# Two reorderings in a fused linear-attention and cosine-gated MLP kernel: an O unit for an F part behind Y of pair 3, and k conversion and T of pair 10 some steps later

## Chip, cores, metric

One core of a Trainium2 chip. The metric is the device time of one launch in microseconds (us), lower is better. All profiles are of that one core.

## The reference, cut to what matters

```python
# q, k, v: (4, 8, 768, 64) fp32; w_in: (512, 2048); w_out: (2048, 512)
for t in range(S):                                   # per batch and head
    state = gamma * state + outer(k[t], v[t])
    y[t] = scale * q[t] @ state
x = y.transpose(0, 2, 1, 3).reshape(3072, 512)
h = x @ w_in
out = (h * cos(h)) @ w_out
```

The kernel does the recurrence in chunks of 128 steps. A *pair* is one chunk of two batches; there are 12, numbered from 0. Two pairs make a *group* of 512 tokens for the MLP. The names used below:

- **conv_k, conv_q, conv_v**: fp32 to bf16, q and v with the decay factors; k on ScalarE, q and v on GpSimd.
- **T**: transposes of q and k, from pair 3 on by DMA.
- **A**: scores of a pair, 16 matmuls into four PSUM banks; VectorE then masks them (`am`).
- **Y, S**: output of the recurrence from masks and state; ScalarE copies it to `xt`. S is the state update.
- **F**: `x @ w_in`, cosine on ScalarE (`cosb`), product on VectorE (`gt`). An F part is 8 matmuls of 128x256, half of what one pair needs for one r, a quarter of `w_in`'s columns; an F unit is 4 of 128x512. From group 2 on a group has 16 steps, each with one F unit.
- **O**: `gt @ w_out`, four units of 4 matmuls make one output tile.

## The kernel before: the parts concerned

```python
banks = Banks([... for i in range(7)], clk)          # seven PSUM banks, one more holds the state
cosb = [sb([128, 4 * C], BF16, f"cosb{i}") for i in range(3)]

def conv_k(p, on_act):
    for b in range(2):
        if on_act:
            nc.scalar.copy(out=qk[p % NB][:, b, 1], in_=kf[SLOT[p]][b])
    ...

def act(bank, out):
    cb = cosb[f_no[0] % 3]                           # cosine buffers in turn
    f_no[0] += 1
    nc.scalar.activation(out=cb, in_=bank, func=AF.Sin, bias=halfpi)
    ...
    nc.vector.tensor_tensor(out=out, in0=bank, in1=cb, op=ALU.mult)
    ...

    # group 1
    pair_f(2, 0)
    conv_k(4, True)
    pair_f(2, 1)
    conv_k(5, True)
    attend(3)                                        # A and masks of pair 3
    cq(4); stage_t_dma(4); cq(5); stage_t_dma(5); cv(4); cv(5)
    fetch_two(6)
    pair_f(2, 2)
    pair_f(2, 3, (0,))
    stage_y(3, nc.scalar.copy)
    pair_f(2, 3, (1,))
    pair_f(3, 0)
    ...
    o_units(1, 0, 2)
    conv_k(6, True)
    attend(4)
    ...
    k_at = {(2, 4): 8, (2, 7): 9, (3, 0): 10, (3, 12): 11}      # (group, step): pair
    t_at = {(2, 8): (8, 9), (3, 2): (10,), (3, 13): (11,)}
    a_at = {(2, 2): 6, (2, 10): 7, (3, 2): 8}

    for g in range(2, NG + 1):
        for s in range(16):
            ...
            if g < NG:
                unit_f(g, s)
            ...  # O unit of the group before, put-off masks
            if at in k_at:
                conv_k(k_at[at], True)
            if at in t_at:
                for p in t_at[at]:
                    cq(p)
                    stage_t_dma(p)
                for p in t_at[at]:
                    cv(p)
                if at == (2, 8):
                    fetch_two(10)                    # loads k, q of 10, k, q of 11, v of 10, 11
            ...
```

## Time and profile before

| | before |
|---|---|
| timed runs | 210.12 us median of 3 (209.74 to 210.32) |
| profiled run | 209.16 us, span 207.2 us |
| TensorE busy, granted clock | 96% of the span, 1.0 |
| ScalarE, VectorE, GpSimd busy | 55%, 54%, 44% |

The granted clock is the share of full TensorE clock that the chip's throttle let through. TensorE is the bound: an engine busy for 96% of the span leaves only its few gaps to win. The prediction below shows the two gaps that the change is aimed at. Part 4 of the page, the chain that ended last, gives shares of the span by engine:

```profile
PE 47%; DMA 10%; POOL 7%; issue 4%; SPq 1%; ACT 1%; DVE 1%; POOLq 0%; ACTq 0%
```

Followed back from the end, the chain is TensorE's for half of the span and then leaves it for loads and GpSimd: somewhere TensorE's end time was set by data coming in, not by its own work. In the timeline lines below, a bracket at the end gives how long the engine stood idle before the instruction, and what ended that.

### The profile page before, as it was taken

What the parts mean: (1) busy time and instruction counts of PE and PEld (TensorE: products, weight loads), DVE (VectorE), ACT (ScalarE), POOL (GpSimd) and SP (SyncE); (2) the same over time, 40 slices, a digit from 0 to 9 for tenths busy, and PEclk for the clock granted to TensorE, in tenths of its full rate; (3) what the DMA queues carried; (4) which work ended last, traced back from release to release, by engine and by line L of the source; (5) the groups of instructions that cost most, each with busy time, mean ns of one, the idle gap of its engine ahead of it and who ended that gap; (6) DMA issues with size and microseconds to landing.
All of it is one profiled execution on the core that took longest, in us unless ns stands there. A gap on an engine that the chain in (4) does not pass through costs nothing.

```text
span 207.2 us, 4072 instructions
## 1 busy us (share of the span) xinstructions
PE 198.4 (96%) x1608; PEld 112.7 (54%) x1630; DVE 112.5 (54%) x186; ACT 114.9 (55%) x193; POOL 92.1 (44%) x99
## 2 busy tenths in 40 slices
PE   7889999999999999999989999999999999999994
PEld 2457554558896555556444465544465444444453
DVE  4792883643967445869574467754458244444000
ACT  6777872259986536787363556453554653554120
POOL 8999238499998389979831630000000000000000
PEclk9999999999999999999999999999999999999999
DMA  6999999989999978999999905101101101110212
GB/s 163 349 237 204 216 252 288 317 186 301 292 158 289 321 106 156 307 295 191 265 365 348 197 3 152 52 3 51 51 0 55 51 0 54 51 51 2 101 51 101
DMA packets 33571, 34.34 MB, mean 166 GB/s; under 512 B 23376, under 2 KB 25680, under 8 KB 33552
## 3 DMA queue, kind: packets, MB, share of 16 engines
q0 software_dynamic: 7824, 22.29, 38.9%
q1 hardware_dynamic: 24544, 11.44, 25.3%
q10 hardware_dynamic: 1184, 0.36, 0.7%
q8 instruction: 12, 0.20, 0.4%
q14 instruction: 7, 0.06, 0.1%
HBM read 27.26 MB, written 6.29 MB: 162 GB/s over the span
## 4 chain that ended last, share of the span: by engine, by line
PE 47%; DMA 10%; POOL 7%; issue 4%; SPq 1%; ACT 1%; DVE 1%; POOLq 0%; ACTq 0%
PE bank L387 24%; PE bank L340 19%; DMA vf<-in_v_dram 4%; DMA qf<-in_q_dram 3%; DMA out_dram<-ob 3%; POOL vs L204 2%; PE bank L407 2%; POOL qk L197 2%; POOL kf L137 2%; POOL qf L137 1%; PE bank L281 1%; PE bank L286 1%; PE bank L259 1%; SPq L380 0%; PE st_ps L303 0%
## 5 line engine op out<-in xcount | busy, mean ns | idle before, releaser
L333 DVE TENSOR_TENSOR gt<-bank,cosb 128x512 bf16<-128x512 f32 x96 | 65.1, 689 | 62.9 <-ACT cosb L329 62.5
L329 ACT ACTIVATE cosb<-bank,halfpi 128x512 bf16<-128x512 f32 x96 | 65.0, 687 | 48.2 <-PE bank L340 42.0
L387 PE MATMUL bank<-w_out_sb,gt 128*128 128x512 bf16 x359 | 88.5, 379 | 0.7 <-issue 0.3
L340 PE MATMUL bank<-xt,w_in 128*128 128x512 bf16 x294 | 74.2, 380 | 1.5 <-DVE gt L333 0.8
L387 PEld LDWEIGHTS <-gt 128*128 128x128 bf16 x368 | 35.5, 98 | 41.2
L340 PEld LDWEIGHTS <-w_in 128*128 128x128 bf16 x304 | 33.8, 114 | 31.6 <-issue 0.8
L268 DVE TENSOR_TENSOR am<-bank,mask 128x512 bf16<-128x512 f32 x48 | 30.4, 682 | 4.4 <-PE bank L259 4.4
L204 POOL TENSOR_TENSOR vs<-vf,gk 128x512 bf16<-128x512 f32 x21 | 21.4, 1049 | 11.6 <-DMA vf<-in_v_dram 8.3
L197 POOL TENSOR_TENSOR qk<-qf,gq 128x512 bf16<-128x512 f32 x18 | 18.4, 1044 | 9.6 <-DMA out_dram<-ob 4.4
L394 ACT COPY ob<-bank 128x512 f32<-128x512 f32 x23 | 13.4, 587 | 16.5 <-PE bank L387 16.3
L210 ACT CAST qk<-kf 128x512 bf16<-128x512 f32 x24 | 13.9, 617 | 12.2 <-DMA kf<-in_k_dram 9.7
L290 ACT CAST xt<-bank 128x512 bf16<-128x512 f32 x24 | 13.0, 589 | 7.1 <-PE bank L286 7.1
L351 PE MATMUL bank<-xt,w_in 128*128 128x256 bf16 x128 | 14.6, 273 | 0.0
L351 PEld LDWEIGHTS <-w_in 128*128 128x128 bf16 x128 | 13.8, 113 | 0.4
L286 PE MATMUL bank<-am,vs 128*64 128x128 bf16 x192 | 11.7, 220 | 0.4 <-DVE am L268 0.4
L281 PEld LDWEIGHTS <-stb 128*64 128x64 bf16 x160 | 8.7, 109 | 4.7 <-issue 4.3
L281 PE MATMUL bank<-qkt,stb 128*64 128x128 bf16 x160 | 10.7, 222 | 0.3 <-DVE am L268 0.3
L137 POOL DMA_DIRECT2D kf<-in_k_dram x9 | 10.6, 1174 | 0.0
L286 PEld LDWEIGHTS <-vs 128*64 128x64 bf16 x192 | 10.0, 110 | 0.5 <-issue 0.4
L315 DVE CAST stb<-st_ps 64x512 bf16<-64x512 f32 x12 | 8.2, 685 | 2.7 <-PE st_ps L303 2.6
L137 POOL DMA_DIRECT2D qf<-in_q_dram x8 | 9.2, 1154 | 0.0
L137 POOL DMA_DIRECT2D vf<-in_v_dram x8 | 9.2, 1152 | 0.0
(48 smaller groups left out, 98.6 us busy)
## 6 DMA issues: line engine op xcount, KB each, us to landing
out_dram<-ob SPq DMA_DIRECT2D x23, 256.0 KB, 2.6
kf<-in_k_dram POOLq DMA_DIRECT2D x9, 512.0 KB, 6.7
qf<-in_q_dram POOLq DMA_DIRECT2D x8, 512.0 KB, 7.1
vf<-in_v_dram POOLq DMA_DIRECT2D x8, 512.0 KB, 8.3
vf<-in_v_dram POOLq DMA_DIRECT2D x8, 256.0 KB, 5.6
w_out_sb<-in_moe_w_out_dram POOLq DMA_DIRECT2D x4, 512.0 KB, 12.2
qf<-in_q_dram POOLq DMA_DIRECT2D x6, 256.0 KB, 7.2
w_in<-in_moe_w_in_dram POOLq DMA_DIRECT2D x3, 512.0 KB, 8.2
```

Of the source, the lines that this page charges most:

```text
L137: nc.gpsimd.dma_start(out=both[n][SLOT[p]].rearrange("p b h d -> p (b h) d"), in_=SRC[n][1][2 * bp : 2 * bp + 2, :, ds(c * C, C)].rearrang ...
L197: eng.tensor_tensor(out=qk[p % NB][:, b, 0], in0=qf[SLOT[p]][b], in1=bc(gq, p % NC), op=ALU.mult)
L204: eng.tensor_tensor(out=vs[p % NB][:, b], in0=vf[SLOT[p]][b], in1=bc(gk, p % NC), op=ALU.mult)
L210: nc.scalar.copy(out=qk[p % NB][:, b, 1], in_=kf[SLOT[p]][b])
L268: nc.vector.tensor_tensor(out=am[p % 2][b][j], in0=ap[j], in1=mask.unsqueeze(1).to_broadcast([128, HP, 128]), op=ALU.mult)
L281: nc.tensor.matmul(yp[ts(j, 64), a, :], lhsT=stb[p % 2][:, b, a, ts(j, 64)], rhs=qt(n, b, a), start=True, stop=False, skip_group_check=True)
L286: nc.tensor.matmul(yp[ts(j, 64), a, :], lhsT=vs[n][:, b, 2 * a + j, :], rhs=am[p % 2][b][j][:, a, :], start=(c == 0), stop=True, skip_grou ...
L329: nc.scalar.activation(out=cb, in_=bank, func=AF.Sin, bias=halfpi)
L333: nc.vector.tensor_tensor(out=out, in0=bank, in1=cb, op=ALU.mult)
L340: nc.tensor.matmul(bank, lhsT=w_in_t(i, f), rhs=xt[g % 2][:, i, :], start=(i == 0), stop=(i == KIN - 1))
L351: nc.tensor.matmul(bank[:, ts(e, 256)], lhsT=w_in_t(i, f + e), rhs=xt[g % 2][:, i, ts(hf, 256)], start=(i == 0 and e == 0), stop=(i == KIN ...
L387: nc.tensor.matmul(bank, lhsT=gt[g % 2][:, f, ts(j, 128)], rhs=w_out_sb[:, f, :], start=(f == 0), stop=(f == KOUT - 1))
```

## The change

The intent: Y of pair 3 should not wait for its masks, and ScalarE should not stand in front of a k that has not landed while finished F units wait behind it.

```diff
     pair_f(2, 2)
-    pair_f(2, 3, (0,))
+    pair_f(2, 3)
     stage_y(3, nc.scalar.copy)
-    pair_f(2, 3, (1,))
+    unit_o(1, 0, 0)
     pair_f(3, 0)
@@
-    o_units(1, 0, 2)
+    o_units(1, 1, 2)
@@
-    k_at = {(2, 4): 8, (2, 7): 9, (3, 0): 10, (3, 12): 11}
-    t_at = {(2, 8): (8, 9), (3, 2): (10,), (3, 13): (11,)}
+    k_at = {(2, 4): 8, (2, 7): 9, (3, 5): 10, (3, 12): 11}
+    t_at = {(2, 8): (8, 9), (3, 6): (10,), (3, 13): (11,)}
```

The first two hunks are *part 1*, the last is *part 2*. Part 2 moves the conversion five steps later and T four.

## The prediction

> **What bounds the kernel now.** I read the page first, then who waited for whom on TensorE, then the timelines of TensorE, ScalarE and VectorE around the two edited places, the chain that ended last, and the landing times of single loads.
>
> ```profile
> PE 198.4 (96%) x1608; PEld 112.7 (54%) x1630; DVE 112.5 (54%) x186; ACT 114.9 (55%) x193; POOL 92.1 (44%) x99
> PEclk9999999999999999999999999999999999999999
> ```
>
> TensorE is busy 96% of a 207.2 us span at full clock; no other engine passes 55%. So the edit can only pay by removing time in which TensorE stands still. Its waits are few:
>
> ```profile
> PE bank L259 <- DVE qkt L216: 1.1, 2, 0.6
> PE bank L340 <- DVE gt L333: 0.8, 1, 0.8
> PE bank L286 <- DVE am L268: 0.4, 1, 0.4
> ```
>
> The first lies in the opening, which is not edited. The other two lie exactly where the diff cuts. The third is in Y of pair 3 (the fourth pair), here in TensorE's timeline (start us, duration us, line, operation, count):
>
> ```profile
> 54.44 0.22 PE L281 MATMUL bank<-qkt,stb 128*64 128x128 bf16 x2
> 54.53 0.22 PE L286 MATMUL bank<-am,vs 128*64 128x128 bf16 x1
> 55.12 0.22 PE L286 MATMUL bank<-am,vs 128*64 128x128 bf16 x1 [0.38 <-DVE am L268]
> ...
> 55.49 0.44 PE L303 MATMUL st_ps<-vs,qk 128*64 128x64 bf16 x16
> ```
> ```profile
> 52.60 2.48 DVE L268 TENSOR_TENSOR am<-bank,mask 128x512 bf16<-128x512 f32 x4
> ```
>
> VectorE's four masks of pair 3 run 52.60 to 55.08. The second half of Y reads the last one, so its first matmul on it starts at 55.12, 0.59 us after its neighbour instead of the usual 0.03. Y and S together take 53.97 to 55.86, 1.89 us; pair 4's, which wait for nothing, take 69.68 to 70.95, 1.27 us. Loss: **0.62 us** (the 0.38 printed starts at the modelled end of the previous matmul).
>
> The second place is the start of group 3. The chain view, in order of time:
>
> ```profile
> 97.34 5.63 DMA out_dram<-ob
> ...
> 103.49 0.61 ACT qk L210
> 104.11 0.59 ACT cosb L329
> ...
> 104.72 0.70 DVE gt L333
> ...
> 105.47 1.02 PE bank L340 x4
> ```
> ```profile
> 99.83 0.69 ACT L329 ACTIVATE cosb<-bank,halfpi 128x512 bf16<-128x512 f32 x1 [0.18 <-PE bank L340]
> 102.97 1.14 ACT L210 CAST qk<-kf 128x512 bf16<-128x512 f32 x2 [2.46 <-DMA out_dram<-ob]
> 104.01 1.26 ACT L329 ACTIVATE cosb<-bank,halfpi 128x512 bf16<-128x512 f32 x2
> ```
>
> ScalarE stands before the k conversion of pair 10 (the eleventh pair) from 100.5 to 102.97. The view blames a store, but the load of k for pair 10 was issued at 95.81 and landed 7.1 us later, at 102.9; that is what the conversion reads. Behind it sit the cosines of the second and third F units of group 3, already computed by TensorE (their matmuls began at 100.49 and 102.21). After the third unit, stage A of pair 8 takes four of the seven PSUM banks, the O unit holds one, and those two F units hold the last two. So the fourth F unit must wait for the second to be evicted: the product ends at 105.42, the matmul starts at 105.47. Stage A started at 104.04 and needs 0.56 us of issue (pair 7's: 92.47 to 93.03), so the F unit could have started at 104.60. Loss: **0.87 us**. From 105.47 to 200.65 the chain is TensorE's own work, apart from one issue gap of 0.17 us.
>
> **What the Trainium skill says.** "PSUM — Partial Sum Buffer", section Engine vs sequencer instructions: the ScalarE, VectorE and GpSimd queues are strictly first in, first out, and matmuls start and finish in program order. The trace agrees: two finished F banks lay behind a conversion that had no data for 2.46 us. The same page, Specifications: 8 banks of 2 KiB, that is 512 fp32 values; the kernel gives one to the state and has seven, which is why stage A's four tell. "TensorE: Matmul & The Clock Gate", Back-to-back issue gap: an isolated gap of about N/2.4 + 2.5 ns, so 216 ns at N=512 and 109 at N=256. The trace agrees: four of N=512 step by 0.86 us. "DMA: Bandwidth & Descriptors", Issuing engines are not separate DMA queues: all issuers share 16 DMA engines and interleave. The trace fits: k of pair 10, loaded while four transposes and eight kept stores ran, took 7.1 us, against 5.3 us for k of pair 8.
>
> **The change, part by part.** No instruction is added or removed. The matmul sum is the same; only order changes.
>
> *Part 1, the F part and the O unit.* Eight matmuls of N=256 (8 x 0.108 = 0.87 us) move from behind Y of pair 3 to in front of it; four of N=512 (4 x 0.216 = 0.86 us) come forward from about 63.7 us to fill the place behind it. Y then starts at 53.97 + 0.87 = 54.84 and its second half at 54.84 + 0.46 = 55.30, after the last mask (55.08; VectorE's order ahead of the masks is unchanged). The wait of 0.62 us goes. A filler is needed because the F parts of pair 3 read xt, which ScalarE copies after Y. New times: Y ends 55.76, S takes 0.37, to 56.13, the O unit 0.87, to 57.0. ScalarE: the displaced cosine 54.9 to 55.6 fits where it idled 0.43 us; the two xt copies then end near 56.1 and 56.6. So the next F part finds xt 0.4 us early. The O unit reads only gt of pair 2's first four F units, long written. It holds one bank through eight F parts; a part holds its bank for 0.86 (matmuls) + 0.69 + 0.69 plus hand-overs, some 2.6 us, so three or four banks, and six are left. Worth **0.62 us at about 57 us**.
>
> *Part 2, conversion and T of pair 10.* Two casts (spacing 0.52 us) move from step 0 to step 5 of group 3, so ScalarE reaches them near 109, six us after k landed: no wait. The cosines follow their matmuls by about 1.1 us and the second unit's bank is free near 103 on the old clock, before 104.60. Worth **0.87 us**. The q conversion on GpSimd waits for q (issued 96.99, landing 10.0 us later; it ran at 107.09), so moving it in the program moves it little. The two DMA transposes started at 108.16 and 110.8 and landed 9.0 and 7.3 us later, at 118.1; now they start some 2 us later, landing near 120 to 121. Their first reader, stage A of pair 10, starts at 129.49 now, about 128.0 then: 7 us to spare.
>
> The sum is 0.62 + 0.87 = **1.49 us**; 210.12 - 1.49 = 208.63, which I round to 208.6.
>
> **Does part 1 survive?** The two parts are not independent. Fetches and their conversions run on GpSimd's own clock (73.1 to 103 us, loads and conversions), whatever TensorE does. With part 1 alone TensorE reaches the start of group 3 earlier by 0.62 us, but k of pair 10 still lands at 102.9, and the fourth F unit still starts near 105.47: part 1 alone should give almost nothing at the end. Part 2 alone should give 0.87; together 1.49.
>
> **Rivals.**
> *Another data wait swallows part 1.* The nearest is k of pair 8: issued 79.16, landed 5.3 us later at 84.46, converted at 84.51 with no slack. TensorE 0.62 us earlier makes ScalarE stand about 0.55 us there. For: zero slack. Against: at that point stage A of pair 6 has released its banks within about 0.6 us, TensorE needs only Y's two, and ScalarE idles 0.2 to 1.0 us before most cosines, so it catches up. If it bites, the gain is 0.9 to 1.2 and the time 209.0 to 209.2.
> *The masks' wait turns into one for xt.* If ScalarE's copies end after 57.0 instead of 56.6, the F part waits: up to 0.3 us lost, 208.9.
> *Conversion or T too late.* If the transposes take longer than 15 us in traffic, stage A of pair 10 waits at 128. They took 2.7 to 9.0 us to land in this trace, and loads end by then. It would cost 1 us or more, 209.6 and up; I give it 4%.
> *The wait is larger in plain runs.* The profiled run took 209.16 us, the three timed ones 209.74 to 210.32. If the extra microsecond is a later landing of k of pair 10, part 2 saves it too and the time is near 207.8.
>
> **Range and chances.** The first two rivals pull up by 0.3 to 0.6, the last pulls down by 0.8, and three runs of before already spread over 0.6. So 207.9 to 209.3 should hold it 8 times in 10. Two per cent is 4.2 us, almost three times the worked-out gain: 98% within, 1% each way.
>
> **What would show it.** In the changed profile: no wait of L286 for am near 55, Y and S of pair 3 in 1.27 us; one O unit between S and the next F; no wait of L340 for gt near 104; ScalarE's conversion of pair 10 after the sixth F unit of group 3 with no DMA wait; a TensorE start of stage A of pair 10 about 1.5 us earlier. I am wrong if L340 waits for ScalarE or VectorE near 57 or 84 to 86, or if stage A of pair 10 waits for its transposes.

## The result, and the profile after

| | before | after |
|---|---|---|
| timed runs | 210.11 us median of 6 (209.15 to 210.32) | 208.51 us median of 6 (208.0 to 208.86) |
| ratio of fast runs | | 0.993 (95%: 0.9907 to 0.9953) |
| span of the profiled run | 207.2 us | 206.7 us |

A ratio is the mean time of one kernel's fast runs over that of the other's of the same rounds, so it is not quite the ratio of the medians quoted beside it. The time is within 0.1 us of the prediction.

The chain of the changed kernel, same line of the page as above:

```profile
PE 87%; DVE 7%; ACT 3%; issue 1%; ACTq 0%; DVEq 0%
```

No DMA and no GpSimd is left in it: from the opening on, TensorE's own work sets the end, but for 4.9 us of VectorE at 53.04 to 57.92 (masks of pair 3 and the products behind them), to which part 1 comes below. That the loads are gone is part 2. At the start of group 3 the changed kernel's TensorE timeline reads:

```profile
104.32 0.62 PE L259 MATMUL bank<-qkt 64*128 64x128 bf16 x16
104.87 1.05 PE L340 MATMUL bank<-xt,w_in 128*128 128x512 bf16 x4
```

From the start of stage A of pair 8 to the next F unit it takes 0.55 us, where before it took 1.43 (104.04 to 105.47): 0.88 us, as predicted. ScalarE's timeline there shows the cosines back in step and the conversion of pair 10 without a wait:

```profile
101.83 0.69 ACT L329 ACTIVATE cosb<-bank,halfpi 128x512 bf16<-128x512 f32 x1 [1.04 <-PE bank L340]
103.56 0.69 ACT L329 ACTIVATE cosb<-bank,halfpi 128x512 bf16<-128x512 f32 x1 [1.04 <-PE bank L340]
...
110.05 1.13 ACT L210 CAST qk<-kf 128x512 bf16<-128x512 f32 x2
```

Part 1 came out differently. TensorE's timeline of the changed kernel behind Y of pair 3:

```profile
56.21 0.42 PE L303 MATMUL st_ps<-vs,qk 128*64 128x64 bf16 x16
56.78 0.81 PE L387 MATMUL bank<-w_out_sb,gt 128*128 128x512 bf16 x3 [0.16 <-issue]
57.91 7.15 PE L351 MATMUL bank<-xt,w_in 128*128 128x256 bf16 x64 [0.32 <-DVE gt L333]
```

Y has no wait for masks any more (55.29 to 56.21, 0.92 us). But the first F part of pair 3 starts at 57.91. S starts at 56.21 and takes about 0.37 us of issue, the O unit 0.87 (one of its four records is missing): TensorE was ready near 57.45, a new wait of about 0.45 us. ScalarE and VectorE of the same kernel show its origin:

```profile
53.30 1.92 ACT L329 ACTIVATE cosb<-bank,halfpi 128x512 bf16<-128x512 f32 x3
56.21 0.69 ACT L329 ACTIVATE cosb<-bank,halfpi 128x512 bf16<-128x512 f32 x1 [1.00 <-DVE gt L333]
56.79 1.07 ACT L290 CAST xt<-bank 128x512 bf16<-128x512 f32 x2
```
```profile
53.04 2.48 DVE L268 TENSOR_TENSOR am<-bank,mask 128x512 bf16<-128x512 f32 x4
55.43 2.47 DVE L333 TENSOR_TENSOR gt<-bank,cosb 128x512 bf16<-128x512 f32 x4
```

There are three cosine buffers. Three cosines fill them from 53.30 on; VectorE can't empty the first before it has done the masks, and its first product ends at about 56.1. So the cosine of the moved F part stands 1.00 us for a buffer. The two xt copies come behind it in ScalarE's order and end at 57.86, and the F part that reads xt starts 0.05 us later. Here the profile names VectorE's last product, which ended at 57.90; the program has that F part wait for both engines, and the experiments tell which.

To measure part 1 without the opening (which ended 0.44 us later in the profiled run of the changed kernel, where no instruction had changed yet), take the time from the start of the F part behind stage A of pair 3 to the start of stage A of pair 4; TensorE has the same work in it in every version. Before: 51.19 to 65.57, 14.38 us. After: 51.63 to 65.85, 14.22 us. The measure repeats where loads come in time: 14.38 in three more traces with the old order (b_only, b_early and before_again), 14.21 in a_only; late loads of k of pairs 4 and 5 make it longer in others. So part 1 gave **0.16 us** instead of 0.62, and the traces account for 0.16 + 0.88 = 1.04 us, less than the 1.5 us that the timed runs show. Both differences are what the experiments are about.

### The profile page after: what moved, and what is told of

Same layout as the page of the kernel before. It is cut to its first block, busy times and chain, and to the rows that moved or that the text cites. A ratio compares the mean times of both kernels' runs of the same rounds, so it can differ in the third digit from the quotient of the medians.

```text
span 206.7 us, 4069 instructions
## 1 busy us (share of the span) xinstructions
PE 198.4 (96%) x1607; PEld 112.6 (54%) x1630; DVE 112.4 (54%) x186; ACT 114.8 (56%) x193; POOL 92.1 (45%) x99
## 4 chain that ended last, share of the span: by engine, by line
PE 87%; DVE 7%; ACT 3%; issue 1%; ACTq 0%; DVEq 0%
PE bank L387 38%; PE bank L340 32%; PE bank L351 4%; DVE am L268 3%; PE bank L281 3%; PE bank L259 2%; PE bank L286 2%; PE bank L407 2%; DVE gt L333 2%; PE st_ps L303 1%; DVE qkt L216 1%; DVE qk L197 1%; PE bank L232 1%; PE bank L362 1%; PE bank L369 1%
## 5 line engine op out<-in xcount | busy, mean ns | idle before, releaser
L340 PE MATMUL bank<-xt,w_in 128*128 128x512 bf16 x294 | 74.3, 380 | 0.7 <-issue 0.3
L340 PEld LDWEIGHTS <-w_in 128*128 128x128 bf16 x304 | 33.7, 114 | 30.9
L351 PE MATMUL bank<-xt,w_in 128*128 128x256 bf16 x128 | 14.5, 273 | 0.3 <-DVE gt L333 0.3
L351 PEld LDWEIGHTS <-w_in 128*128 128x128 bf16 x128 | 13.9, 113 | 1.1 <-issue 0.6
```

What stands on the lines that cost most here:

```text
L340: nc.tensor.matmul(bank, lhsT=w_in_t(i, f), rhs=xt[g % 2][:, i, :], start=(i == 0), stop=(i == KIN - 1))
L351: nc.tensor.matmul(bank[:, ts(e, 256)], lhsT=w_in_t(i, f + e), rhs=xt[g % 2][:, i, ts(hf, 256)], start=(i == 0 and e == 0), stop=(i == KIN ...
```

## The experiments

All kernels gave correct results. Kernels of one batch ran on the same chip, another chip in each batch, and share 11 runs of the kernel before.

| batch | kernel | median us (range, 6 runs) | ratio to before (95%) |
|---|---|---|---|
| 1 | before | 209.95 (208.64 to 211.98) | |
| 1 | a_only | 209.81 (208.56 to 214.82) | 0.9994 (0.9944 to 1.0044) |
| 1 | b_only | 208.63 (208.16 to 209.63) | 0.9957 (0.9917 to 0.9997) |
| 1 | both_cosb4 | 207.84 (207.5 to 208.81) | 0.9921 (0.9879 to 0.9963) |
| 1 | before_again | 209.47 (208.82 to 212.12) | 0.9983 (0.9942 to 1.0024) |
| 2 | before | 210.45 (209.5 to 212.94) | |
| 2 | after_again | 208.74 (208.13 to 209.09) | 0.9897 (0.9844 to 0.995) |
| 2 | two_o | 208.24 (207.69 to 209.16) | 0.9881 (0.9832 to 0.9931) |
| 2 | b_early | 208.73 (208.34 to 209.09) | 0.9898 (0.9851 to 0.9945) |
| 2 | k_load_early | 208.8 (208.14 to 209.56) | 0.9901 (0.9851 to 0.995) |
| 3 | before | 209.5 (208.56 to 212.44) | |
| 3 | both_cosb4_2 | 208.12 (207.62 to 208.84) | 0.9948 (0.9922 to 0.9974) |
| 3 | a_cosb4 | 209.17 (208.37 to 210.42) | 0.9996 (0.996 to 1.0032) |
| 3 | b_cosb4 | 208.74 (208.14 to 209.72) | 0.998 (0.9949 to 1.001) |
| 3 | k5_later | 208.32 (207.77 to 209.95) | 0.9965 (0.993 to 1.0) |

Ratios use fast runs alone: a run over 1.5% above the fastest of its kernel is called slow. The medians and ranges take in the slow ones: two, one and one of before, one of before_again (212.12) and one of a_only (214.82), whose five fast runs have a median of 209.17. The kernel before scatters by 3 to 4 us within a batch (2.1 to 2.9 in its fast runs) and its median moves by 1 us between batches, while the others move by 0.1 to 0.3; so versions are compared with each other inside a batch by their medians. The fast runs of one version still spread over 0.7 to 2.2 us, so a difference of 0.5 us between two medians is weak by itself; there the traces decide.

### Each part alone

**a_only**: part 1 alone (the first two hunks of the change).

> Part 1 alone (F part ahead of Y of pair 3, O unit behind it). Theory T: k of pair 10 lands at a time that TensorE does not set (102.9 us), so a gain made at 57 us is eaten at the start of group 3: change against before between -0.2 and +0.1 us, and in the trace the fourth F unit of group 3 still starts within 0.2 us of k's landing plus 2.5 us. Rival A (the gains simply add): -0.6 us if the prediction's size holds, -0.17 us if the trace of the changed kernel does (0.62 saved at the masks, 0.45 lost at xt). In the trace, counted from Y's start to the next F part: no wait for masks, a wait of about 0.45 us ahead of the first F part of pair 3.

Measured: no change that the runs can tell, ratio 0.9994; the interval is some 1 us to either side and both theories lie in it. In its trace part 1 gives 0.17 us (51.18 to 65.39, 14.21 us), and the fourth F unit starts at 105.02, the conversion of pair 10 having started, on k's landing, at 102.52: 2.50 us later. In the kernel before it was 102.97 and 105.47: 2.50. This fits theory T, but 0.17 us are too few to be sure against a scatter of 2 us in the runs; a_cosb4 below asks again with the full size.

**b_only**: part 2 alone (the last hunk).

> Part 2 alone (conversion and T of pair 10 later). Theory T: -0.87 us as read from the trace of before, and the wait for masks near 55 us stays at 0.62 us. Rival: plain runs of before wait longer than its profiled run did (the changed kernel gained 1.5 us in the timed runs, while its trace shows 0.17 + 0.88); then -1.2 to -1.5 us.

Measured: ratio 0.9957, in the middle some 0.9 us; by medians 1.3 us. Its trace has no wait at the start of group 3, and the one for the masks (0.4 us as printed) is there. In the trace nearly the whole gain of the change is in this part: 0.88 of 1.04 us.

**a_cosb4**: part 1 alone with a fourth cosine buffer.

```diff
-    cosb = [sb([128, 4 * C], BF16, f"cosb{i}") for i in range(3)]
+    cosb = [sb([128, 4 * C], BF16, f"cosb{i}") for i in range(4)]
-        cb = cosb[f_no[0] % 3]
+        cb = cosb[f_no[0] % 4]
```

> Part 1 alone with the fourth cosine buffer, which makes part 1 worth its full 0.6 us at 57 us. Theory T: k of pair 10 lands when it lands, so the wait at the fourth F unit of group 3 grows by what was gained before it (to some 1.4 us where k lands at 102.9), and the time stays that of before within 0.3 us, or gets worse in runs in which the gap grows past 2 us. Rival A (gains add): 0.6 us below before.

Measured: ratio 0.9996, no gain, but the interval (0.8 us of gain to 0.7 of loss) does not exclude the 0.6 us of rival A; the trace has to decide. TensorE's and ScalarE's timelines of this kernel at the start of group 3:

```profile
103.64 0.62 PE L259 MATMUL bank<-qkt 64*128 64x128 bf16 x16
105.71 1.02 PE L340 MATMUL bank<-xt,w_in 128*128 128x512 bf16 x4 [1.45 <-DVE gt L333]
```
```profile
103.21 1.14 ACT L210 CAST qk<-kf 128x512 bf16<-128x512 f32 x2 [3.10 <-DMA out_dram<-ob]
```

Stage A comes 0.40 us earlier than in the kernel before, and the wait behind it is longer: 1.45 us printed, against 0.81. (It is 0.40 and not 0.6 because in this run k of pair 5 came late: ScalarE stood 0.72 us for it, and the stretch of part 1 took 14.00 us, 0.38 less than before.) Of the 0.64 us of longer wait, 0.40 is the earlier arrival and 0.24 k's later landing. Again the F unit starts 2.50 us after the conversion does. What is gained ahead of a load that lands when it lands is handed back at the load. In the trace theory T stands and rival A falls; the times alone would leave both. The runs did not get worse either: the longer wait showed no tail here (up to 210.42).

### Why part 1 was worth so little

**both_cosb4**: the changed kernel with the four buffers of the diff above.

> The changed kernel with a fourth cosine buffer. Theory C: the new wait ahead of the first F part of pair 3 comes from the cosine of the moved F part, which needs a buffer that VectorE frees only after the masks; with four buffers the cosine starts near 55.3 instead of 56.2 us and the xt copies end 0.4 to 0.9 us earlier, the wait of 0.45 us goes: 0.35 to 0.5 us below the changed kernel, so about -1.9 us against before. Rival: the PSUM bank of that F part is what is late (the profile names VectorE's product); then a cosine buffer changes nothing there and the time is that of the changed kernel, -1.5 us.

Measured: 207.84 us, 0.8 below b_only of the same batch (the changed kernel itself was not run in it, so the buffer's own gain is read from the traces). ScalarE, then VectorE, then TensorE, of this kernel:

```profile
55.13 0.69 ACT L329 ACTIVATE cosb<-bank,halfpi 128x512 bf16<-128x512 f32 x1 [0.23 <-ACT cosb L329]
55.71 1.06 ACT L290 CAST xt<-bank 128x512 bf16<-128x512 f32 x2
```
```profile
55.11 2.47 DVE L333 TENSOR_TENSOR gt<-bank,cosb 128x512 bf16<-128x512 f32 x4
```
```profile
56.24 1.04 PE L387 MATMUL bank<-w_out_sb,gt 128*128 128x512 bf16 x4
57.11 7.15 PE L351 MATMUL bank<-xt,w_in 128*128 128x256 bf16 x64
```

The cosine no longer stands for a buffer, the xt copies end at 56.77, before TensorE needs them, and the F part follows the O unit in 0.87 us, with no wait. From F part to stage A of pair 4: 51.31 to 65.06, 13.75 us, 0.63 less than before. That is the 0.62 of the prediction. The buffer was the cause of the 0.45 us lost; the bank was not: here VectorE's last product, which empties that bank, ends at 57.58, and the F part has started at 57.11 without it.

**both_cosb4_2**: the same kernel again.

> The changed kernel with a fourth cosine buffer once more, beside the next three: median 207.5 to 208.1 us (its first was 207.84), and in its trace no wait ahead of the first F part of pair 3.

Measured: 208.12 us, 13.75 us on the same stretch (51.16 to 64.91), and no wait there. The median is just outside what was expected.

**b_cosb4**: part 2 alone with the fourth buffer.

> Part 2 alone with the fourth cosine buffer. Theory C: the fourth buffer helps only through the moved F part; where the order of Y and F is as before it gives nothing: the time of part 2 alone (208.6), 0.5 to 0.9 us above part 1, part 2 and the buffer together, with the wait for masks near 55 us back in the trace. Rival: the buffer helps elsewhere too, then it lies within 0.3 us of the two parts with the buffer.

Measured: 208.74 us, the time of part 2 alone (208.63 and, for its two cousins below, 208.73 and 208.8), 0.62 above both_cosb4_2 of the same batch, and the wait for masks (0.4 us printed) is back in its trace. By these medians and traces the buffer helps through the moved F part alone; the difference of 0.62 is not far outside the scatter.

**two_o**: two O units behind Y instead of one; three buffers.

```diff
     unit_o(1, 0, 0)
+    unit_o(1, 0, 1)
     pair_f(3, 0)
@@
-    o_units(1, 1, 2)
```

> The changed kernel with two O units behind Y of pair 3 instead of one (the second is drawn ahead of the first F part of pair 3, no buffer added). Theory X: that F part waits for the xt copies, which end 0.40 us after the one O unit does; a second unit of 0.86 us covers the whole wait, so 0.4 to 0.5 us below the changed kernel, as the fourth cosine buffer gave, and the cosine of the moved F part still waits 1.0 us for its buffer. Rival: the bank or the buffer itself holds TensorE up later on, then less than 0.2 us.

Measured: 208.24 us, 0.50 below after_again of the same batch, the size expected; but the means are only 0.3 apart and the ranges overlap, so the trace carries this. On TensorE:

```profile
56.45 1.90 PE L387 MATMUL bank<-w_out_sb,gt 128*128 128x512 bf16 x8
58.19 7.15 PE L351 MATMUL bank<-xt,w_in 128*128 128x256 bf16 x64
```

Eight O matmuls and then F without a wait; the stretch takes 51.53 to 65.27, 13.74 us, as with four buffers. The xt copies in this run ended at 57.75, behind the end of the first O unit (57.32) and ahead of that of the second. One miss: the cosine stood 0.48 us for its buffer, not 1.0, as ScalarE itself was 0.46 us late there (next heading but one). So the same loss can be repaired by a buffer or by enough other work in front of it.

### Which wait part 2 removes

**b_early**: the conversion of pair 10 only one step later.

```diff
-    k_at = {(2, 4): 8, (2, 7): 9, (3, 0): 10, (3, 12): 11}
+    k_at = {(2, 4): 8, (2, 7): 9, (3, 1): 10, (3, 12): 11}
```

> Kernel before with the k conversion of pair 10 only one step later, behind the cosine of the second F unit of group 3 (step 1 instead of 0), T where it was. Theory P: the fourth F unit waits for the bank of the second one alone, so putting that one cosine ahead of the conversion is enough: ScalarE still stands 1 to 1.5 us for k, but TensorE does not wait at the fourth F unit; the whole gain of part 2, -0.8 to -1.0 us, comes back. Rival: the conversion must be clear of the landing by half a group; then the wait moves to the next F unit and less than half of the gain comes.

Measured: 208.73 us, the same as after_again (208.74). ScalarE, then TensorE, of this kernel:

```profile
101.53 0.69 ACT L329 ACTIVATE cosb<-bank,halfpi 128x512 bf16<-128x512 f32 x1 [1.04 <-PE bank L340]
102.78 1.14 ACT L210 CAST qk<-kf 128x512 bf16<-128x512 f32 x2 [0.56 <-DMA kf<-in_k_dram]
103.82 0.68 ACT L329 ACTIVATE cosb<-bank,halfpi 128x512 bf16<-128x512 f32 x1
```
```profile
104.02 0.62 PE L259 MATMUL bank<-qkt 64*128 64x128 bf16 x16
104.57 1.05 PE L340 MATMUL bank<-xt,w_in 128*128 128x512 bf16 x4
```

ScalarE still stands for k, for 0.56 us (less than the 1 to 1.5 expected, since the cosine in front now fills part of the time), and TensorE does not notice. It is one cosine, and through it one PSUM bank, that had to get past the conversion. Five steps are more room than this needed in this run. In the run-to-run tail that room might still pay; that was not tested.

**k_load_early**: conversion and T left alone, the load of k moved forward on GpSimd.

```diff
                     stage_t_dma(p)
+                if at == (2, 8):
+                    load_both(("k", 10))
                 for p in t_at[at]:
                     cv(p)
                 if at == (2, 8):
-                    fetch_two(10)
+                    load_both(("q", 10), ("k", 11), ("q", 11), ("v", 10), ("v", 11))
```

> Kernel before with the load of k for pair 10 issued ahead of the four v conversions of pairs 8 and 9 on GpSimd, some 4 us earlier; conversion and T stay where they were. Theory T: what ScalarE waits for is this load, not the store that the profile names; it lands near 98 to 99 us, before the conversion is reached at 100.5, and the wait goes: -0.8 to -1.0 us. Rival: the conversion waits for the stores or transposes whose end the profile shows at 102.97; then nothing changes, 0 +- 0.2 us.

Measured: 208.8 us. The load is issued at 92.67 and lands 6.4 us later, at 99.1; the conversion follows the first cosine with no wait in ScalarE's timeline:

```profile
101.09 1.13 ACT L210 CAST qk<-kf 128x512 bf16<-128x512 f32 x2
```

So it was this load that ScalarE waited for, not the store (`out_dram<-ob`) that the views of the kernel before name; the store only ended at the same time. Here the stores were issued from 98.89 on and took 5.9 us or more to land, so the conversion at 101.09 ran before any of them had.

### The scatter, and a repair that failed

**before_again**: the kernel before, unchanged.

> The kernel before once more, as a control and for a second profile. Time within 0.2 us of before. Theory R: the landing of k of pair 10 scatters from run to run: its wait at the fourth F unit of group 3 differs by some tenths from the 0.87 us of the first profile, and a run with a longer wait is longer by as much. Rival: the wait is the same within 0.1 us and the runs differ in the opening (first transposes at 5.1 us against 5.3 us in the profile of the changed kernel).

Measured: 209.47 us, and a second profile, of a run of 212.12 us. Its first steps are no later than in the first profile. At the start of group 3 TensorE shows

```profile
106.79 1.65 PE L340 MATMUL bank<-xt,w_in 128*128 128x512 bf16 x4 [2.13 <-DVE gt L333]
```

k's load was issued at 96.75 instead of 95.81 and took 7.5 us instead of 7.1; the conversion started at 104.28, the F unit 2.51 us later. So the landing, and with it the wait, does scatter: 102.52, 102.97, 103.21 and 104.28 in the four traces with the conversion at step 0, and always 2.50 or 2.51 us to the F unit. The windows of that run show one thing more (time, PE busy, PEld, DVE, ACT, POOL, then granted clock, DMA share, GB/s):

```profile
106.00:108.00 2.00, 1.21 (x4) 0.53 (x4) 1.96 (x4) 0.59 (x2) 1.07 (x2) 0.76 1.04 364
108.00:110.00 2.00, 2.00 (x7) 0.67 (x5) 1.33 (x3) 0.69 (x1) 0.98 (x1) 0.50 1.05 366
110.00:112.00 2.00, 2.00 (x10) 0.92 (x9) 1.10 (x3) 1.27 (x2) 0.00 (x0) 0.89 1.03 362
```

Behind the gap of 2.13 us the granted clock went down to 0.50 and came back by 112. Of the 3.0 us by which this span exceeds the first profile's, the longer wait is 1.32 (106.79 less 105.47) and the rest, 1.68, is lost by stage A of pair 9 at the latest (it starts at 123.64 instead of 120.64). In fact three units of four matmuls, which step by 0.86 us elsewhere, took 1.44, 1.71 and 1.12 us just there (starts at 106.79, 108.23, 109.94 and 111.06): that is the 1.68. It is one run, slow, so it explains no difference between the kernels here.

The mean clocks for the other executions point the same way. Of 51 with the conversion at step 0 and the load in its old place (before, before_again, a_only, a_cosb4), seven have a mean clock of 0.984 to 0.991, and they take 211.98 to 214.82 us; five of them count as slow. Of 60 executions of the kernels in whose traces the fourth F unit does not wait (every other one of this document), none is below 0.997. So taking the wait away may also take away a lower clock behind it, in about one run of seven. Only one of the seven has a trace, so this is not shown.

**after_again**: the changed kernel, unchanged.

> The changed kernel once more, on the same chip and against the same runs of before as the three that follow: ratio 0.991 to 0.996 to before (its first was 0.993), about 0.2 us below part 2 alone as its traces say (0.62 saved at the masks, 0.45 lost at xt).

Measured: ratio 0.9897, a little better than the interval that was expected, because the kernel before was slower in this batch (two of its fast runs, both of 212.09 us, are among those with a clock of 0.99). Against b_early, which has part 2 in its smallest form, it gained nothing (208.74 and 208.73): part 1's 0.16 us drown in the scatter. Its trace has a wait that the first one had not, 0.47 us ahead of an F part at 52.77. Such a wait appears in k_load_early, b_cosb4 and k5_later as well, 0.49 to 0.57 us, where loads of k of pairs 4 and 5 land late.

**k5_later**: with four buffers, the conversion and T of pair 5 behind one more r of F parts.

```diff
     pair_f(2, 1)
-    conv_k(5, True)
     attend(3)
@@
     cq(5)
-    stage_t_dma(5)
     cv(4)
@@
     pair_f(2, 2)
+    conv_k(5, True)
+    stage_t_dma(5)
     pair_f(2, 3)
```

> The changed kernel with the fourth cosine buffer and with the k conversion and T of pair 5 behind one more r of F parts (two F parts later on ScalarE). In some executions ScalarE stood 0.46 to 0.53 us for k of pair 5 near 52 us, and TensorE 0.47 to 0.57 us behind it. Theory D: this wait makes part of the scatter of the changed kernel; moved out of the way, the median falls by 0.1 to 0.4 us below the two parts with the buffer and the spread narrows. Rival: T of pair 5 then comes too late for stage A of pair 5, or VectorE's products hold banks longer: slower by 0.3 us or more.

Measured: 208.32 us against 208.12 of both_cosb4_2, no gain, and a spread that is wider, not narrower. Theory D was not tested by it, as the wait was not moved out of the way: the profiled run still waits 0.49 us ahead of the F part at 52.74, and on ScalarE the k that is late is that of pair 4:

```profile
50.23 1.14 ACT L210 CAST qk<-kf 128x512 bf16<-128x512 f32 x2 [0.49 <-DMA kf<-in_k_dram]
```

I had moved the wrong conversion for this run. Whether this wait makes part of the scatter, and what moving both conversions would do, is open.

## Why the prediction was right, point by point

- **The time** (208.6 predicted, 208.51 measured) is right, but in part by luck: the traces account for 1.04 us of the 1.49, because part 1 came out 0.46 short, and a difference of about the same size in the timed runs, whose cause is open, made up for it.
- **Part 2** (0.87): the mechanism and the size hold in the trace (0.88), and b_early and k_load_early show it by two other ways of taking the same wait away. What it is worth in the timed runs is less sure: before less the kernel with part 2 alone, in its various forms, is 1.3 us in batch 1, 1.7 in batch 2 and 0.8 in batch 3 by medians, and 0.9, 2.1 and 0.4 by the ratios of fast runs, the last with an interval that takes in zero. The fourth rival ("The wait is larger in plain runs") says that it is worth more there than in the trace. The four traces show that the wait does move, with a landing that differs by up to 1.8 us (one of the four is slow); that it explains the difference is likely, not shown, since no traces of the other runs were kept.
- **Part 1** (0.62): the term that was mis-sized; it measured 0.16. The masks' wait went away as said. The step that failed is "the displaced cosine 54.9 to 55.6 fits where it idled 0.43 us; the two xt copies then end near 56.1 and 56.6". I counted ScalarE's idle time and PSUM banks, and not the three cosine buffers: the cosine started at 56.21 and the copies ended at 57.86. The second rival named this wait for xt and put it at up to 0.3 us; it was 0.45. (The sign named for it, a wait of L340 near 57, has the line of the F units; the F parts are L351, and there it showed.) With a fourth buffer the sum for ScalarE holds: the copies end at 56.77 in a run whose opening was 0.12 later, against 56.6.
- **Does part 1 survive**: right, by the traces. Alone it gave nothing that the runs can tell (0.9994 with three buffers, 0.9996 with four, intervals of 0.4 to 0.5% to either side), and the delay from landing to the F unit stayed at 2.50 us. Together with part 2 and the fourth buffer its full size comes through: 0.6 to 0.8 us between both_cosb4 and part 2 alone.
- **The first rival** (k of pair 8) did not bite: that conversion ran at 84.74 in the changed kernel without a wait. **The third** (T too late) did not either: the transposes of pair 10 started at 110.73 and landed at most 5.8 us after their issue (the second near 117.4), some 11 us ahead of stage A of pair 10, at 128.92. That stage came 0.57 us earlier in the trace, not 1.5; 0.44 of the difference is the later opening of that run and 0.46 is part 1.

The best version of batches 1 and 3 is the changed kernel with a fourth cosine buffer: 207.84 and 208.12 us, 0.6 us or more below part 2 alone in both. two_o, the best of batch 2, was not run beside it.

## What to carry to other kernels

A gain made ahead of a load that lands at its own time is handed back at the load: find the last such wait downstream and remove it first, or with it. When a unit of work is moved forward, walk through every ring of buffers on its way (banks, scratch tiles), and ask which engine frees the next one and what stands in that engine's queue. And let what blocks an in-order engine stand behind the one instruction that others wait for: one step was enough in the run traced here.

## What the Trainium skill lacked or had wrong

- "Perfetto Trace Analysis", Identifying Performance Opportunities, speaks of consistent bubbles as a sign of too few buffers. Here too few buffers made a single gap of 0.45 us, two engines away from the buffer: cosine (1.00 us for its buffer), xt copies, F part. A fourth buffer took it away (14.22 to 13.75 us on the stretch).
- "TensorE: Matmul & The Clock Gate", Why this matters for your kernels, advises no idle gaps over some 3 us. In one run a gap of 2.13 us was followed by granted clocks of 0.76, 0.50 and 0.89 in windows of 2 us; after one of 1.45 us, in a_cosb4, the clock stayed at 1.00. One slow run, so an observation only.
- "TensorE: Matmul & The Clock Gate", Back-to-back issue gap, from which the prediction takes its formula, says more than the prediction tells: it gives about 131 ns per matmul at N=512 for a stream of weight loads and matmuls, and calls the formula's 216 too high for it. Here the formula holds in the stream itself, at a granted clock of 1.0: four of N=512 step by 0.86 us, 216 ns each, and 64 of N=256 took 57.11 to 64.10 in both_cosb4, 109 ns each.
- No page says how far the landing of one load scatters between runs of a kernel: the conversion that waits for k of pair 10 started at 102.97 and at 104.28 us in two runs of the same kernel, and the wait behind it was 0.81 and 2.13 us. Of the 1.31 us between the two, 0.94 is GpSimd issuing the load later (95.81 and 96.75) and 0.4 the load itself (7.1 and 7.5 us); the second run is slow.
